# One shift per tile of patterns and Mish's first instruction on GpSimd, O in two buffers, and a newly planned order

## The chip, the cores and the metric

The kernel runs on one core of a Trainium2 chip. The metric is the device time of one execution in microseconds (us), the median of several runs. Five engines work in parallel, each in its own fixed order, held together by semaphores: TensorE (PE in the profile, PEld for its weight loads), VectorE (DVE), ScalarE (ACT), GpSimd (POOL) and SyncE (SP), which issues most DMAs.

## The reference

The input is a sequence of S = 2048 tokens of width D = 640. Two branches are computed from it and mixed by a gate for each token.

```python
def _A_ref(x, wqkv, wo):                      # attention, H = 32 heads of Dh = 20
    qkv = (x @ wqkv).reshape(B, S, 3, H, Dh)  # q, k, v: [B, H, S, Dh]
    scores = einsum("bhqd,bhkd->bhqk", q, k) * Dh ** -0.5
    p = softmax(scores, axis=-1)
    o = einsum("bhqk,bhkd->bhqd", p, v)
    return o.transpose(0, 2, 1, 3).reshape(B, S, D) @ wo

def _B_ref(x, w1, b1, w2):                    # dense layer with Mish, F = 1536
    h = einsum("bsd,df->bsf", x, w1) + b1
    act = h * tanh(softplus(h))
    return einsum("bsf,fd->bsd", act, w2)

g = sigmoid((x * gate_w).sum(-1, keepdims=True))
return g * a + (1 - g) * b
```

All inputs are bf16.

## The kernel before

**Blocks.** The attention weights are cut into blocks of 128 keys x 512 queries of one head. There are 32 heads x 16 key tiles x 4 query chunks = 2048 such blocks. PE computes a block of scores into PSUM (L1219); then the block has to go through an exponential, and PE multiplies it with V (L1456). Four heads of a group and a key tile make a *tile* of four blocks.

**Two ways to an exponential.** ACT takes two or three blocks in one instruction and writes bf16 (L1246: 128x1024 is a *pair*, 128x1536 a *triple*). DVE takes whole tiles. It turns each score into a 16-bit integer by one multiplication and addition (L1304, one instruction for each of four blocks), and those bits, read as a half-precision number, are a rough exponential. To make it a good one, three such *patterns* are summed with weights: two more copies of the tile are made by adding a constant to all its integers (L1334, one instruction of 128x2048 int16 for each copy; the text calls it a *shift*). PE multiplies the three patterns with V, with V x 161/128 and with V x 203/128. These two scaled sets of V are made by GpSimd (L1359, two instructions of 128x84 for each tile). So a tile of patterns costs DVE six instructions, and PE three passes over it in place of one.

**After a group.** When a group of four heads and a query chunk is done, DVE copies its output O with the sums of the softmax from PSUM into one buffer OUNG (L1551). The sums go by DMA to RR, are inverted there (L1558), and go by two more DMAs (L1559, L1561) to all partitions of BCT; then GpSimd multiplies O with them in four pieces of 128x128 (L1518). The next copy into OUNG waits for these.

**Mish.** The other branch runs in the background of the attention. For each of 24 pieces of 128x1024, ACT takes one tanh (L1013) and DVE does the rest in six instructions (L1033 to L1038): the *lift* (L1033, float32 to half precision), two cheap additions (L1034, L1036) and three products (L1035, L1037, L1038).

**What sets the order.** The Python code plans the whole program before it is built. A table of constants gives each kind of instruction a cost. The planner walks through steps (a step is one ACT exponential), and at each one decides from the planned clocks of the engines what every engine does next: whether a tile is taken for patterns (`start_tile`), which queue DVE serves (`work`: norm, soon, blend, bg), when PE does a background matmul. `STRETCHES` replaces some of the constants from given steps on. What comes out is one fixed list of instructions for each engine, with waits on semaphores; nothing is decided on the chip. At the start three of the four query chunks of x are loaded by transposing DMAs (L557), two ahead of the bulk of the weights (L582) and one behind them.

A second program, for inputs whose scores could leave the range of the patterns, is built too and not executed here.

Of the kernel before, what the change touches and what calls it, by code (L numbers as in the profile page):

```python
# [17 lines left out]
P = 128  # L18
# [41 lines left out]
HALVED = 0.41  # L60
# [7 lines left out]
Q_WAIT = 6  # L68
# [7 lines left out]
TIMES = 0.7  # L76
# [13 lines left out]
MISH = 1.7  # L90
# [4 lines left out]
FULL = 0.60  # L95
SCALED = 0.34
LIFT = 512.0
# [13 lines left out]
CALM = 6  # L111
PACKED = 17
# [18 lines left out]
SETS = 8  # L131
ULPS = 1024 / math.log(2)
BASE = 13680.1
SHADE = 0.61


STRETCHES = {
    13: {"EAGER": 144, "FMIN": 0.128, "FREE": 0.235, "SPUN": 0.495, "THIRD": 1.187, "VMIN": 1.48},
    33: {"EAGER": 144, "FMIN": 0.273, "FREE": 0.235, "SPUN": 0.495, "THIRD": 1.187, "VMIN": 1.48},
    53: {"CALLED": 7.573, "CALM": 3, "EAGER": 144, "FMIN": 0.332, "FREE": 0.235, "PATIENCE": 11.967, "ROOM": 2.116, "SPUN": 0.495, "THIRD": 1.187, "VMIN": 1.48, "XLATE": 10.107, "XSLACK": 0.076},  # L140
    74: {"AHEAD": 32, "CALLED": 7.573, "CALM": 8, "CROWD": 1.442, "EAGER": 144, "FMIN": 0.354, "FREE": 0.235, "NEED": 2, "OVER": 0.266, "PATIENCE": 3.941, "ROOM": 2.116, "SPUN": 0.467, "THIRD": 1.341, "VMIN": 1.48, "XLATE": 10.107, "XSLACK": 0.076},
    95: {"BUSY": 1.495, "CALLED": 2.701, "CROWD": 1.338, "FMIN": 0.33, "FREE": 0.173, "SPUN": 0.564, "STREAM": 0.496},
    116: {"CROWD": 1.454, "ROOM": 1.78, "STREAM": 0.464, "VMIN": 0.691, "XSLACK": 0.385},
    138: {"CROWD": 1.454, "EAGER": 159, "FREE": 0.15, "ROOM": 1.78, "STREAM": 0.464, "THIRD": 0.562, "VMIN": 0.691, "XSLACK": 0.385},
    159: {"XSLACK": 0.541},
    178: {"AHEAD": 13, "BEHIND": 21.412, "BUSY": 0.268, "CROWD": 1.246, "EAGER": 144, "FREE": 0.235, "MARGIN": 1.043, "OVER": 0.25, "PATIENCE": 12.851, "ROOM": 2.303, "XSLACK": 0.56},
    197: {"AHEAD": 17, "BEHIND": 13.21, "BUSY": 0.268, "CALLED": 2.332, "CALM": 9, "CROWD": 1.378, "EAGER": 144, "FMIN": 0.062, "FREE": 0.148, "LATER": 0.62, "MARGIN": 1.043, "OVER": 0.279, "PATIENCE": 8.968, "ROOM": 2.303, "XSLACK": 0.56},
    218: {"AHEAD": 17, "BEHIND": 13.21, "BUSY": 0.268, "CALLED": 2.332, "CALM": 9, "CROWD": 1.378, "EAGER": 156, "FMIN": 0.062, "FREE": 0.148, "KEPT": 14, "LATER": 0.62, "LOAD": 0.609, "MARGIN": 1.043, "OVER": 0.279, "PATIENCE": 13.444, "ROOM": 2.078, "STREAM": 0.365, "XLATE": 7.955, "XSLACK": 0.633},
    238: {"BUSY": 0.481, "EAGER": 131, "FMIN": 0.093, "LATER": 0.493, "LOAD": 0.49, "MARGIN": 0.871, "ROOM": 2.374, "XSLACK": 0.42},
    259: {"BUSY": 0.481, "CALLED": 1.571, "EAGER": 131, "FMIN": 0.065, "LATER": 0.493, "LOAD": 0.49, "MARGIN": 0.871, "NEED": 4, "OVER": 0.166, "ROOM": 2.345, "STREAM": 0.348, "VMIN": 2.036, "XSLACK": 0.42},  # L150
# [135 lines left out]
def bass_gated_mix__softmax_full_mha__dense_activation_mish__prompt_kernel(  # L286
# [39 lines left out]
    U2 = sb("U2", [P, 2 * CW], FP32)  # L326
    RR = sb("RR", [P, 16], FP32)
    BCT = sb("BCT", [P, CW], FP32)
    GATE = sb("GATE", [P, NTB], FP32)
    OMG = sb("OMG", [P, NTB], FP32)  # L330
    GT1 = sb("GT1", [P, NTB], FP32)
# [77 lines left out]
    def attention(pl, fast):  # L409
# [42 lines left out]
        def real(g):  # L452
            return min(g, NG - 1)
# [1553 lines left out]
```

## Time and profile before

| | |
|---|---|
| median of 3 runs | 752.26 us (752.16 to 753.0) |
| the profiled execution's own time | 752.22 us |
| its span | 750.3 us |
| mean granted clock of TensorE | 0.997 |
| DMA | 50.44 MB, mean 67 GB/s |
| work of the start (0 to 12 us) | ACT busy 6.47 us, DVE 5.02 us |
| the middle (32 to 700 us) | ACT busy 666.15 us, DVE 631.55, PE 653.19, POOL 187.32 |

A row of the groups reads: line, engine, operation, output <- inputs, (partitions x elements, type) and count | busy us, mean ns of one | idle time of the engine just before, and what ended it. Consecutive instructions of one engine overlap a little at their ends, so that a mean duration is somewhat longer than the distance from start to start. The busy time of PE is modelled, and 96% there does not mean that PE is at its peak.

### The profile page before, as it was taken

The page shows a single profiled execution, that of the slowest core. Times are in us where ns is not written, and L with a number is a line of the kernel's source. Part 1 is how long each engine was busy: PE and PEld are TensorE (multiplying, and loading weights), DVE is VectorE, ACT ScalarE, POOL GpSimd, SP SyncE. Part 2 cuts the span into 40 slices and gives each one's busy share as a digit, 9 for nine tenths or more (in the row PEclk, how much of TensorE's full clock was granted, in tenths as well). Part 3 has the DMA queues.
Part 4 walks back from the last instruction along what each step waited for, and adds up shares of the span by engine and source line. Part 5 has one row for each costly group of instructions (what it writes and reads, how often), then busy time and mean ns, then how long its engine had stood idle before and what let it go on. Part 6 is the DMA issues. An engine that isn't in the chain of part 4 may idle for free.

```text
span 750.3 us, 25694 instructions
## 1 busy us (share of the span) xinstructions
PE 721.5 (96%) x11307; PEld 274.8 (37%) x11307; DVE 689.9 (92%) x1203; ACT 732.8 (98%) x764; POOL 211.8 (28%) x399
## 2 busy tenths in 40 slices
PE   8899999999999999999989999999999999999996
PEld 3333334334423342233333433334444434333342
DVE  3698898999999999998999999999999999999986
ACT  6899999999999999999999999999999999999995
POOL 3203241312332213232213332212331243313142
PEclk9999999999999999999999999999999999999998
DMA  9402422132233313632132111111212212010001
GB/s 235 61 26 70 83 85 85 26 112 64 57 93 119 94 56 88 181 70 54 41 86 74 56 34 30 43 43 56 87 52 70 68 58 70 21 30 21 30 17 42
DMA packets 78015, 50.44 MB, mean 67 GB/s; under 512 B 21408, under 2 KB 73880, under 8 KB 77848
## 3 DMA queue, kind: packets, MB, share of 16 engines
q1 hardware_dynamic: 75528, 48.24, 23.3%
q8 instruction: 91, 1.49, 0.9%
q10 hardware_dynamic: 2256, 0.47, 0.3%
q14 instruction: 28, 0.23, 0.1%
q0 software_dynamic: 112, 0.01, 0.1%
HBM read 39.01 MB, written 8.90 MB: 64 GB/s over the span
## 4 chain that ended last, share of the span: by engine, by line
ACT 63%; PE 18%; DVE 11%; DMA 4%; SPq 1%; issue 1%; POOL 0%; DVEq 0%
ACT ETS L1246 62%; PE PS L508 6%; PE PS L1219 6%; PE PS L1456 5%; DVE LN L1304 3%; DVE LN L1334 2%; DMA XB<-in_A_x_dram 2%; SPq L557 1%; ACT REG L1013 1%; DMA W2R<-in_B_w_dram 1%; DMA BCT<-SUMS 1%; DVE REG L1304 1%; DVE HB L989 1%; DMA RR<-OUNG 1%; ACT W2R L1013 1%
## 5 line engine op out<-in xcount | busy, mean ns | idle before, releaser
L1246 ACT ACTIVATE ETS<-PS 128x1024 bf16<-128x1024 f32 (+1 forms) x733 | 711.2, 1158 | 3.8 <-PE PS L1219 3.1
L1219 PE MATMUL PS<-QT,KT 32*128 32x512 bf16 (+1 forms) x2128 | 287.6, 377 | 14.0 <-ACT ETS L1246 10.5
L1304 DVE TENSOR_SCALAR LN<-PS 128x512 int16<-128x512 f32 x396 | 266.1, 682 | 25.0 <-PE PS L1219 23.6
L1518 POOL TENSOR_TENSOR QT<-OUNG,BCT 128x128 bf16<-128x128 f32 x124 | 65.9, 562 | 481.6 <-DMA BCT<-SUMS 481.6
L1219 PEld LDWEIGHTS PS<-QT,KT 32*128 32x128 bf16 x2128 | 72.3, 91 | 238.9 <-ACT ETS L1246 211.5
L1359 POOL TENSOR_SCALAR VS<-V_all 128x84 bf16<-128x84 bf16 x262 | 138.9, 530 | 35.9 <-DVE V_all L836 8.0
L1456 PE MATMUL PS<-ETS,V_all 128*21 128x512 bf16 (+1 forms) x1596 | 148.0, 375 | 0.1
L1334 DVE TENSOR_SCALAR LN<-LN 128x2048 int16<-128x2048 int16 x182 | 126.1, 695 | 3.7 <-PE PS L1456 3.1
L508 PE MATMUL PS<-XB,REG 128*32 128x256 bf16 (+2 forms) x1800 | 87.2, 296 | 2.7 <-DVE LN L1304 1.8
L1456 PE MATMUL PS<-LN,VS 128*21 128x512 f16 (+1 forms) x832 | 78.7, 379 | 0.3
L508 PE MATMUL PS<-W2R,HB 128*32 128x320 bf16 x1536 | 74.4, 301 | 0.0
L1456 PEld LDWEIGHTS PS<-ETS,V_all 128*21 128x21 bf16 x1596 | 37.8, 90 | 50.4 <-issue 42.2
L508 PEld LDWEIGHTS PS<-XB,REG 128*32 128x32 bf16 (+1 forms) x1800 | 41.7, 96 | 29.9 <-issue 19.4
L508 PE MATMUL PS<-WOQ,QT 128*32 128x320 bf16 x1024 | 50.7, 301 | 0.6 <-DVE QT L1544 0.5
L508 PEld LDWEIGHTS PS<-W2R,HB 128*32 128x32 bf16 x1536 | 35.8, 96 | 24.2 <-issue 12.2
L1304 DVE TENSOR_SCALAR REG<-PS 128x512 int16<-128x512 f32 x60 | 40.1, 679 | 1.5 <-PE PS L1219 1.2
L1456 PE MATMUL PS<-LN,V_all 128*21 128x512 f16 (+1 forms) x408 | 38.7, 376 | 0.2 <-DVE OUNG L1551 0.2
L508 PE MATMUL PS<-XB,WOQ 128*32 128x512 bf16 (+2 forms) x440 | 35.5, 382 | 0.3 <-DVE LN L1304 0.3
L1456 PEld LDWEIGHTS PS<-LN,VS 128*21 128x21 bf16 x832 | 19.7, 89 | 39.9 <-issue 21.6
L989 DVE TENSOR_TENSOR HB<-PS,B1F 128x512 bf16<-128x512 f32 x48 | 32.6, 679 | 0.5 <-PE PS L508 0.4
L508 PEld LDWEIGHTS PS<-WOQ,QT 128*32 128x32 bf16 x1024 | 23.2, 96 | 17.3 <-issue 8.7
L1304 DVE TENSOR_SCALAR W2R<-PS 128x512 int16<-128x512 f32 x36 | 24.2, 682 | 0.6 <-PE PS L1219 0.6
(116 smaller groups left out, 496.8 us busy)
## 6 DMA issues: line engine op xcount, KB each, us to landing
REG<-in_B_w_dram SPq DMA_DIRECT2D x36, 320.0 KB, 3.3
BCT<-SUMS SPq DMA_DIRECT2D x31, 256.0 KB
W2R<-in_B_w_dram SPq DMA_DIRECT2D x12, 320.0 KB, 4.2
QT<-QS SPq DMA_DIRECT2D x28, 128.0 KB, 3.3
KT<-KS SPq DMA_DIRECT2D x28, 128.0 KB
KS<-LN SPq DMA_DIRECT2D x16, 128.0 KB, 3.4
QS<-WOQ SPq DMA_DIRECT2D x16, 120.0 KB
W2R<-in_B_w_dram SPq DMA_DIRECT2D x12, 160.0 KB, 3.8
```

Source lines behind the costliest of these rows:

```text
L508: last = e.matmul(to[at + j:at + j + n, :], w[:, j:j + n], x, start=start, stop=stop, tile_position=(0, at + j))
L557: "sp", lambda e: e.dma_start_transpose(xt(c), x_ap[c * CW:(c + 1) * CW, :]), (), f"xt{c}", cost=4.5, tail=3.6)]
L989: ev = dve(lambda e: e.tensor_tensor(hb, PS[:, bank, :].rearrange("p (i t) -> p i t", i=2), bias, ALU.add), [last, *b1f, *guarded, *b_read ...
L1013: ex = pl.add("act", lambda e: e.activation(U, h, AF.Tanh, bias=BEND, scale=0.5), [ev, u_free[0]], cost=0.94)
L1219: op = pl.add("pe", lambda e, to=to, g=real(g), tile=tile, j=j, cols=cols, c=c, of_q=of_q: e.matmul(to[:, cols], KT[32 * j:32 * j + 32, g, ...
L1246: e_op[s] = pl.add("act", lambda e: e.activation(RING[:, p:p + n, :], scores(s)[:, 0:n, :], AF.Exp, scale=SCALE), [s_op[s], *(pv_slot[b] f ...
L1304: bank_free[bank] = x_ops[bank] = tile["op"] = dve(lambda e: e.tensor_scalar(dst, PS[:, bank, :], SCALE * ULPS, BASE, ALU.mult, ALU.add), ...
L1334: op = pl.add("dve", lambda e: e.tensor_scalar(to, src, SHADES[n] - SHADES[held], None, ALU.add), [made, *deps], cost=SHADE)
L1359: weighted[(c, g, k)] = n, [pl.add("pool", lambda e, i=i, n=n, src=src: e.tensor_scalar(VS[:, n, i, :, :], src, WEIGHTS[i + 1], None, ALU. ...
L1456: lasts[n] = pl.add("pe", lambda e, v=v, j=j, src=src[:, cols], of_q=of_q, begin=begin, end=end: e.matmul(PS[32 * j:32 * j + EW, ACC, of_q ...
L1518: oung_free[0] = bc_read[0] = otn_done[(c, g)] = pl.add("pool", lambda e, some=some: e.tensor_tensor(otn(c, g)[:, some], src[:, some], BC[ ...
```

## The change

What it does:

- The second shift of each tile moves from DVE to GpSimd, as two instructions of 128x1024 (`GLOOM = 2`). The first stays on DVE. The patterns may now be made and used in either order.
- Mish's lift moves from DVE to GpSimd, in four pieces of 128x256 (`LIFTER = 1`). The other five instructions stay on DVE. GpSimd's work is put in order by a new function, `grind`.
- O is copied into two buffers of OUNG in turn.
- The sets of scaled V are 5 instead of 8. Some small tensors share memory.
- All three transposing loads of x go ahead of the bulk of the weights.
- The constants of the planner and all of `STRETCHES` are new, and with them the order of the program. It now takes 139 tiles for patterns (556 blocks) where it took 127 (508 blocks), and ACT's 733 exponentials are 707 pairs and 26 triples where they were 659 and 74.

```diff
-SETS = 8
+SETS = 5
+LIFTED = 0.43
+HOMES = {0: ('dve', 1024, FULL), 1: ('pool', 256, 0.4), 2: ('pool', 128, 0.27), 3: ('pool', 256, 0.69), 4: ('pool', 128, 0.42)}
+LIFTER, MILLER, ENDER = 1, 0, 0
+SPLIT = 1
+GLOOM = 2
+SHADOW = 2.25
...
-    OUNG = sb("OUNG", [P, CW], FP32)
+    OUNG = sb("OUNG", [P, 2, CW], FP32)
...
-            load_x(1)
-            load_x(2)
+            for c in range(1, NC):
+                load_x(c)
...
-            load_x(3)
...
+            def grind():
+
+                while gloom and pl.now["pool"] < pl.now["act"] + GRIST:
+                    if gloom[0][0]().t1 + HOP >= pl.now["act"] + AWAY:
+                        break
+                    gloom.popleft()[1]()
+                while mill and mill[0][0].t1 + HOP < pl.now["act"] + AWAY and pl.now["pool"] < pl.now["act"] + GRIST:
+                    mill.popleft()[1]()
...
+                    w = HG // count
+                    for i in range(count):
+                        some = slice(i * w, (i + 1) * w)
+                        op = pl.add(eng, lambda e, some=some: e.tensor_scalar(
+                            to[:, some, :], src[:, some, :], SHADES[n] - SHADES[held], None, ALU.add), [made, *deps], cost=cost)
...
-            for n in range(1, len(SHADES)):
-                piece(n)
+            if not GLOOM:
+                for n in range(1, len(SHADES)):
+                    soon.append((SHADE, piece(n, "dve", 1, SHADE), ready, due))
+            else:
+                soon.append((SHADE, piece(1, "dve", 1, SHADE), ready, due))
+                gloom.append((ready, piece(2, "pool", GLOOM, SHADOW / GLOOM + 0.1)))
...
-            while oung_free[0] == "busy":
+            m = oung_turn[0]
+            oung_turn[0] = 1 - m
+            while oung_free[m] == "busy":
                 (norm or lasting).popleft()[1]()
-            src = OUNG[:, :]
+            src = OUNG[:, m, :]
```

Of `STRETCHES` one line shows the kind of change:

```diff
-    546: {"OVER": 0.225, "ROOM": 1.348},
+    536: {"CROWD": 1.522, "FMIN": 0.103, "LATER": 0.57, "LOAD": 0.578, "XSLACK": 0.335},
```

In the changed kernel the lines are: exponential L1295, conversion to patterns L1353, shift L1388 (on both engines), scaled V L1420, copy of O L1621, scaling of O L1586, lift L1043, Mish's products L1044 and L1045, its additions L1048, its tanh L1029.

**On DVE, around the twelfth of the 24 pieces of Mish.** Before (U2 holds the half-precision numbers of Mish, LN and REG patterns):

```order
L1033 TENSOR_SCALAR U2<-REG 128x1024
L1304 TENSOR_SCALAR REG<-PS 128x512
L1034 TENSOR_SCALAR U2<-U2 128x1024
L1075 SCALAR_TENSOR_TENSOR REG<-PS,GATE,XS 128x320
L1035 TENSOR_TENSOR U2<-U2 128x1024
L1334 TENSOR_SCALAR LN<-LN 128x2048
L1036 TENSOR_SCALAR U2<-U2 128x1024
L1304 TENSOR_SCALAR LN<-PS 128x512
L1037 TENSOR_TENSOR U2<-U2 128x1024
L1075 SCALAR_TENSOR_TENSOR REG<-PS,GATE,XS 128x320
L1038 TENSOR_TENSOR HB<-U2,HB 128x1024
```

And now:

```order
L1048 TENSOR_SCALAR U2<-U2 128x1024
L1353 TENSOR_SCALAR LN<-PS 128x512
L1044 TENSOR_TENSOR U2<-U2 128x1024
L1048 TENSOR_SCALAR U2<-U2 128x1024
L1353 TENSOR_SCALAR LN<-PS 128x512
L1124 SCALAR_TENSOR_TENSOR REG<-PS,GATE,XB 128x320
L1005 TENSOR_TENSOR HB<-PS,B1F 128x512
L1353 TENSOR_SCALAR LN<-PS 128x512
L1044 TENSOR_TENSOR U2<-U2 128x1024
L1353 TENSOR_SCALAR LN<-PS 128x512
L1621 COPY OUNG<-PS 128x512
```

The lift at the head is gone from DVE, and conversions from PSUM (L1353) stand where shifts and the lift stood.

**On GpSimd, between two scalings of O in the middle of the program.** Before:

```order
L1518 TENSOR_TENSOR QT<-OUNG,BCT 128x128 x4
L1359 TENSOR_SCALAR VS<-V_all 128x84 x8
L1518 TENSOR_TENSOR QT<-OUNG,BCT 128x128 x4
L1359 TENSOR_SCALAR VS<-V_all 128x84 x10
L1518 TENSOR_TENSOR QT<-OUNG,BCT 128x128 x4
```

And now:

```order
L1586 TENSOR_TENSOR QT<-OUNG,BCT 128x128 x4
L1388 TENSOR_SCALAR REG<-LN 128x1024 x2
L1420 TENSOR_SCALAR VS<-V_all 128x84 x2
L1388 TENSOR_SCALAR LN<-LN 128x1024 x2
L1420 TENSOR_SCALAR VS<-V_all 128x84 x2
L1388 TENSOR_SCALAR REG<-LN 128x1024 x2
L1420 TENSOR_SCALAR VS<-V_all 128x84 x2
L1388 TENSOR_SCALAR LN<-LN 128x1024 x2
L1420 TENSOR_SCALAR VS<-V_all 128x84 x2
L1043 TENSOR_SCALAR U<-REG 128x256 x4
L1388 TENSOR_SCALAR LN<-LN 128x1024 x2
L1420 TENSOR_SCALAR VS<-V_all 128x84 x2
```

Where GpSimd had eight or ten small instructions in one piece and then waited for the next scaling of O, it now has two large shifts between each two small ones, and the scaling of O stands in line behind them.

**On ACT, from the fourteenth tanh of Mish on** (all rows but L1013 and L1029 are exponentials). Before:

```order
L1013 ACTIVATE REG<-HB 128x1024
L1246 ACTIVATE ETS<-PS 128x1024 x3
L1246 ACTIVATE ETS<-PS 128x1536
L1246 ACTIVATE ETS<-PS 128x1024
L1246 ACTIVATE ETS<-PS 128x1536
L1246 ACTIVATE ETS<-PS 128x1024 x3
L1246 ACTIVATE ETS<-PS 128x1536
L1246 ACTIVATE ETS<-PS 128x1024 x10
L1013 ACTIVATE REG<-HB 128x1024
```

And now:

```order
L1029 ACTIVATE REG<-HB 128x1024
L1295 ACTIVATE ETS<-PS 128x1024 x47
L1029 ACTIVATE REG<-HB 128x1024
L1295 ACTIVATE ETS<-PS 128x1024 x15
L1029 ACTIVATE REG<-HB 128x1024
```

The triples are gone from this part; only pairs are left.

More of the change, by code (lines that the diff above doesn't have):

```diff
@@ L111 @@
 CALM = 6
+HANG = 2.0
 PACKED = 17
@@ new lines, in plus @@
+                def plus(s):
+                    return lambda e, at: e.tensor_scalar(B[:, at], A[:, at], 1 / LIFT, s, ALU.mult, ALU.add)
+                chains.append((ex, due, [
+                    (*HOMES[LIFTER], lift, taken), ("dve", 2 * CW, SCALED, plus(a - 2), None), (*HOMES[MILLER], times, None),
+                    ("dve", 2 * CW, SCALED, plus(b - c), None), (*HOMES[MILLER], times, None), (*HOMES[ENDER], last, done)]))
+                if len(chains) == 1:
+                    onward(ex, 0)
@@ L1470, in sets @@
             for tile in off_tiles.get(queue[0][2][:2], ()):
[L1471 removed]
+                n += sum(op.t1 + HOP <= pl.now["pe"] for op, *_ in tile["items"][tile["given"]:])
             return n
```

243 lines of the change are left out of this document (138 added, 105 removed).

## The prediction

> **What bounds the kernel now.** First the page's busy times, then its chain of work that ended last.
>
> ```profile
> span 750.3 us, 25694 instructions
> PE 721.5 (96%) x11307; PEld 274.8 (37%) x11307; DVE 689.9 (92%) x1203; ACT 732.8 (98%) x764; POOL 211.8 (28%) x399
> ...
> ACT 63%; PE 18%; DVE 11%; DMA 4%; SPq 1%; issue 1%; POOL 0%; DVEq 0%
> ```
>
> ACT is busy for all but 17.5 us of the span, and most of the chain runs on it. So the time is the sum of ACT's instructions plus a start and an end. DVE has some 60 us free, GpSimd more than 500. The groups of instructions with their shapes kept apart say what ACT's time is made of:
>
> ```profile
> L1246 ACT ACTIVATE ETS<-PS 128x1024 bf16<-128x1024 f32 x659 | 624.8, 1115 | 3.0 <-PE PS L1219 2.2 <-PE PS L1456 0.2
> L1246 ACT ACTIVATE ETS<-PS 128x1536 bf16<-128x1536 f32 x74 | 113.1, 1540 | 0.9 <-PE PS L1219 0.9
> ```
>
> A triple takes 1.540 us, a pair 1.115, and ACT waited less than 4 us for work. What ACT does not take, DVE must take as patterns, so the change buys ACT time with DVE time, and DVE time with GpSimd time. The waits of the engines show how much lateness lies between DVE and ACT:
>
> ```profile
> PEld PS L1219 <- ACT ETS L1246: 211.5, 583, 1.3
> ...
> DVE LN L1304 <- PE PS L1219: 23.6, 54, 2.7
> ...
> ACT ETS L1246 <- PE PS L1219: 3.1, 6, 1.0
> ```
>
> PE, which stands between them, waited 583 times for ACT to free a PSUM bank, 0.36 us on average. A delay of PE by DVE that is shorter than this does not reach ACT.
>
> **The change, part by part.** The working is against the profiled execution: 752.22 us, of which 750.3 are its span and 1.9 lie around it. That is the median of the runs (752.26).
>
> *ACT.* There are 733 exponentials as before, but 48 triples have become pairs. Each saves 1.540 - 1.115 = 0.425 us, so 48 x 0.425 = **20.4 us**, all on the path. With nothing else changed this gives 752.2 - 20.4 = 731.8 us.
>
> *DVE.* It gets 48 more conversions and loses 115 shifts (254 to 139) and the 24 lifts:
>
> ```profile
> L1304 DVE TENSOR_SCALAR LN<-PS 128x512 int16<-128x512 f32 x396 | 266.1, 682 | 25.0 <-PE PS L1219 23.6
> L1334 DVE TENSOR_SCALAR LN<-LN 128x2048 int16<-128x2048 int16 x182 | 126.1, 695 | 3.7 <-PE PS L1456 3.1
> L1033 DVE TENSOR_SCALAR U<-REG 128x1024 f16<-128x1024 f32 x18 | 12.3, 682 | 0.0
> L1033 DVE TENSOR_SCALAR U<-W2R 128x1024 f16<-128x1024 f32 x6 | 4.6, 760 | 0.0
> ```
>
> That is 48 x 0.682 = 32.7 more, 115 x 0.695 = 79.9 and 12.3 + 4.6 = 16.9 less: 689.9 - 64.1 = 625.8 us of work.
>
> *PE.* Twelve more tiles of three passes instead of one are 24 passes of four matmuls. A row of the timeline (start, duration) gives what one costs:
>
> ```profile
> 300.70 0.40 PE L1456 MATMUL PS<-LN,VS 128*21 128x512 f16 x4
> ...
> 300.93 0.39 PE L1456 MATMUL PS<-LN,V_all 128*21 128x512 f16 x4
> ```
>
> They start 0.23 us apart, so this is 5.5 us, hidden by the 211.5 us in which PE waits for ACT. Without that cover it would be 5.5 us.
>
> *GpSimd.* The trace has no shift there. These rows have the nearest things:
>
> ```profile
> L1359 POOL TENSOR_SCALAR VS<-V_all 128x84 bf16<-128x84 bf16 x262 | 138.9, 530 | 35.9 <-DVE V_all L836 8.0
> ...
> L591 POOL COPY WOQ<-WOQ 128x400 bf16<-128x400 bf16 x1 | 0.5, 517 | 3.5 <-DMA WOQ<-in_A_wqkv_dram 3.5
> ...
> L607 POOL COPY REG<-GW 128x5 bf16<-128x5 bf16 x1 | 0.2, 207 | 4.0 <-DMA GW<-in_gate_w_dram 4.0
> ...
> L1874 POOL TENSOR_TENSOR HB<-LN,W2R 128x320 bf16<-128x320 f32 x1 | 0.9, 857 | 7.8 <-ACT LN L1872 7.8
> ```
>
> ```profile
> L1359 POOL TENSOR_SCALAR VS<-V_all x262: 417/418/1441, 17.3 to 735.7; 128x84 bf16<-128x84 bf16 x131
> ...
> L1518 POOL TENSOR_TENSOR QT<-OUNG,BCT x124: 447/457/1178, 57.0 to 733.6; 128x128 bf16<-128x128 f32 x124
> ```
>
> ```profile
> 145.87 1.70 POOL L1518 TENSOR_TENSOR QT<-OUNG,BCT 128x128 bf16<-128x128 f32 x4 [10.75 <-DMA BCT<-SUMS]
> 147.66 0.92 POOL L1359 TENSOR_SCALAR VS<-V_all 128x84 bf16<-128x84 bf16 x2
> ```
>
> The two copies differ by 395 elements and 310 ns: 0.785 ns for an element of one input. The 128x84 instruction takes 418 ns at its median, so 418 - 84 x 0.785 = 352 ns of it are fixed. A half shift is then 0.352 + 1024 x 0.785 ns = 1.16 us, and 1.24 from start to start (a pair of the small ones in the third fence: 0.92 - 0.42 = 0.50, which is 0.08 more than one takes). The other end is the slope of the two-input instruction, (857 - 457) / 192 = 2.1 ns, which gives 2.58 us. The shift has one input, so I take 1.24. A lift of 128x256 by the same rule is 0.63. GpSimd's sum: 278 x 1.24 = 345, 282 small ones x 0.50 = 141, 124 scalings x 0.42 = 52, 96 lifts x 0.63 = 61, some 10 at the start: **609 us**, 83% of the new span. It fits, with 120 us to spare.
>
> *DVE against GpSimd.* The two engines get in each other's way. The groups of line 1334 and two pairs of rows of the timeline:
>
> ```profile
> L1334 DVE TENSOR_SCALAR W2R<-W2R x12: 676/684/990, 48.3 to 272.3; 128x2048 int16<-128x2048 int16 x12
> ```
>
> ```profile
> 673.85 0.97 DVE L1334 TENSOR_SCALAR REG<-REG 128x2048 int16<-128x2048 int16 x1
> ```
>
> ```profile
> 673.81 0.46 POOL L1518 TENSOR_TENSOR QT<-OUNG,BCT 128x128 bf16<-128x128 f32 x1 [15.69 <-DMA BCT<-SUMS]
> ```
>
> ```profile
> 606.22 0.68 DVE L1334 TENSOR_SCALAR LN<-LN 128x2048 int16<-128x2048 int16 x1
> ```
>
> ```profile
> 606.05 0.95 POOL L1359 TENSOR_SCALAR VS<-V_all 128x84 bf16<-128x84 bf16 x1
> ```
>
> At 673.8 a shift that begins just behind a scaling of O takes 0.97 instead of 0.68: it waits 0.29 us, about 128 elements at 2.1 ns. At 606 the small instruction had begun 0.17 us ahead of the shift; the shift is not delayed, but GpSimd takes 0.95 instead of 0.42. So one waits for the other only while elements move, not in GpSimd's fixed part, and a half shift holds DVE back for up to 1024 x 0.785 ns = 0.80 us.
>
> The Trainium skill ("SBUF — State Buffer", § SBUF: two separate sides) says that these engines share a port pair as an exclusive lock, and that whoever starts first holds it for the whole instruction. The rows agree with the exclusion; the pair at 606 disagrees with "starts first" and with "whole". By that rule GpSimd would hold the ports for 278 x 1.16 + 282 x 0.42 + 124 x 0.46 + 96 x 0.55 = 550 us, DVE would lose 84 us instead of the 34 worked out next, and the sum would be some 744 us; the sum goes by the rows.
>
> GpSimd moves elements for 278 x 0.80 + 124 x 0.29 + 96 x 0.20 + 282 x 0.07 = 297 us, 41% of 730. A DVE instruction that comes at a random moment waits with that chance, on average for 0.32 us (half of what it hits, most of it 0.80). DVE has 139 shifts, 48 additions and 72 products of Mish that can be held up: 259 x 0.41 x 0.32 = **34 us**. So DVE works 625.8 + 34 = 660 of 730 us, and has 70 us free where it had 60: it is no tighter than before. What reaches ACT is the part of a wait that exceeds PE's 0.36 us. Of 259 x 0.41 = 106 waits spread over 0 to 0.80 us this is 0.12 us each, 13 us if PE needs every delayed result at once, and nothing if the planner left slack everywhere. I take **5 us**, since a shift is mostly followed by conversions into banks that PE needs later.
>
> *New waits.* Mish's first addition on DVE now waits for GpSimd's lift, whose four pieces take 4 x 0.63 = 2.5 us instead of 0.68; 24 times 1.8 us of lateness in background work, with nothing behind it that is due at once. A shift on DVE that writes over the tile it came from waits until GpSimd has read that tile; conversions stand behind it, and PE waits for those: this is what the upper end of 13 us is for. The scalings of O wait for a DMA at the head of GpSimd's queue, and now shifts stand behind them:
>
> ```profile
> POOL QT L1518 <- DMA BCT<-SUMS: 481.6, 31, 28.0
> ```
>
> Before, nothing stood behind those 31 waits that was due. If each still costs 1 us, 31 us of the 120 spare ones are gone, and nothing of ACT's time.
>
> *Small parts.* The second buffer of O saves one wait, and covers the scalings that now stand behind shifts; 0 to -0.8 us, taken as 0:
>
> ```profile
> DVE OUNG L1551 <- POOL QT L1518: 0.8, 1, 0.8
> ```
>
> The third load of x goes ahead of three issues of weights on SP (first fence, SP's timeline). The chain at the start waits for its arrival (second fence):
>
> ```profile
> 10.04 0.58 SPq L582 DMA_DIRECT2D REG<-in_A_wqkv_dram  x1
> 10.66 0.53 SPq L582 DMA_DIRECT2D WOQ<-in_A_wqkv_dram  x1
> 11.23 0.75 SPq L582 DMA_DIRECT2D REG<-in_A_wqkv_dram  x1
> ```
>
> ```profile
> 12.03 12.70 DMA XB<-in_A_x_dram
> ```
>
> 0.58 + 0.53 + 0.75 = 1.9: it can gain up to 1.9 us, and lose as much if the weights come late; taken as 0. Fewer sets of V only mean that they are made just before they are used; GpSimd's spare time covers this.
>
> **Sum:** 752.2 - 20.4 + 5 = 736.8 us. With the bounds (-1.9 - 0.8 at the start and the buffer, 0 to 13 for the waits): 729 to 745.
>
> **Rivals.**
>
> 1. *DVE becomes the bound, and the kernel is slower.* Both shifts of a tile wait for the same fourth conversion, so DVE's and GpSimd's start together, and each of the 139 would meet a half shift in full: 139 x 0.80 = 111 us, and 120 x 0.41 x 0.32 = 16 for Mish. DVE would need 626 + 127 = 753 us beside the 15 us of the first 32 in which it has no work yet:
>
> ```profile
> 0.00:12.00 12.00, 8.75 (x128) 4.14 (x132) 5.02 (x12) 6.47 (x9) 5.85 (x11) 1.00 1.01 190
> 12.00:32.00 20.00, 18.02 (x268) 7.57 (x264) 11.57 (x20) 18.38 (x20) 6.16 (x13) 1.00 0.72 163
> ```
>
> (The third pair of numbers is DVE: 5.02 of 12 us and 11.57 of 20.) It decides at a mean wait of 0.43 us: 626 + 259 x 0.43 + 15 = 752 us. For it speaks that rows such as the one at 673.8 exist; against it that in the new order of DVE a shift stands between conversions, so that its turn is rarely the very moment at which its tile is ready. At 0.46 us, with the 1.9 us around the span: 626 + 119 + 15 + 2 = about **762 us**. The Trainium skill ("Perfetto Trace Analysis", § Optimizing Scalar/DVE Operations) warns in the same sense that moving work between these two engines might not help because of the shared port.
>
> 2. *GpSimd becomes the bound.* With c for a half shift its sum is 264 + 278 c. At c = 1.6 this is 709 us, beside its own waits for DVE (those of the 0.95 us kind, some 30 us) more than the span. The third pattern then comes late for PE, and PE's fixed order stops ACT. At c = 1.8: 264 + 500 + 30 = 794 us. For it: the slope of 2.1 ns in the row of L1874. Against it: that row has two inputs.
>
> 3. *Most of the gain is eaten.* The waits come as single delays up to 0.8 us, and PE's fixed order passes them on more often than I take: the 13 us, and 3 more where GpSimd's third pattern comes late. 731.8 + 16 = **748 us**, still faster.
>
> 4. *Nothing comes of it:* the 20.4 us come back as waits of ACT for PE, 752 us.
>
> **How the numbers follow.** My forecast (729 to 745) gets 0.60, rival 3 0.14, rival 4 0.05, rival 1 0.13, rival 2 0.08. About 0.2%, 1.5 us, is what a measurement of this kernel can tell from no change. Faster by more: 0.60 + 0.14 = 0.74; the same: 0.05; slower: 0.21. The range that holds 8 in 10 takes the forecast, rival 3 and rival 4: 729 to 753.
>
> **What would show it.** Right: about 707 pairs at 1.115 us and ACT busy for some 712 us; half shifts on POOL at 1.1 to 1.3 us and POOL at 80 to 90%; L1388 on DVE with a median near 0.69 and a maximum near 1.5; DVE's busy time, waits included, 645 to 675. Wrong by rival 1: a mean of L1388 on DVE above 1.1 us and PE waiting for DVE. Wrong by rival 2: POOL above 95% and PE waiting for POOL at L1524. Wrong altogether: ACT waiting for PE for more than 20 us.

## The result and the profile after

| | before | after |
|---|---|---|
| median | 752.21 us (752.16 to 753.0) | 1147.64 us (1145.2 to 1150.45) |
| ratio | | 1.5254, 95% interval 1.5217 to 1.5291 |
| profiled execution: span | 750.3 us | 1143.2 us |
| mean granted clock of TensorE | 0.997 | 0.824 |

The prediction, 736.8 us in a range of 729 to 753, was wrong, in sign as well as in size. The page of the changed kernel begins with the busy times:

```profile
span 1143.2 us, 26026 instructions
PE 883.3 (77%) x11376; PEld 297.3 (26%) x11377; DVE 705.8 (62%) x1112; ACT 749.2 (66%) x764; POOL 1028.7 (90%) x795
```

ACT has gone from 98% of the span to 66%, GpSimd (POOL) from 28% to 90%. The groups say with what, and the durations of one group (minimum/median/maximum in ns, first and last start) how long one is:

```profile
L1388 POOL TENSOR_SCALAR LN<-LN 128x1024 int16<-128x1024 int16 x170 | 480.0, 2841 | 25.6 <-DVE LN L1353 25.4 <-PE PS L1524 0.2
L1420 POOL TENSOR_SCALAR VS<-V_all 128x84 bf16<-128x84 bf16 x282 | 145.6, 516 | 23.9 <-DVE V_all L851 1.6
L1586 POOL TENSOR_TENSOR QT<-OUNG,BCT 128x128 bf16<-128x128 f32 x124 | 57.8, 495 | 0.1
```

```profile
L1388 POOL TENSOR_SCALAR LN<-LN x170: 2760/2772/3286, 30.4 to 1095.1; 128x1024 int16<-128x1024 int16 x170
```

A half shift takes **2.77 us**, not 1.24. The 170 of this group are most of the 278; all of them need 278 x 2.77 = 770 us. The waits show how that reaches ACT:

```profile
ACT ETS L1295 <- PE PS L1268: 365.2, 279, 6.6
PEld PS L1524 <- POOL LN L1388: 216.7, 94, 6.0
DVE LN L1353 <- PE PS L1268: 203.1, 210, 6.3
PE PS L1524 <- POOL LN L1388: 187.6, 88, 5.7
```

Read from below: PE comes to the third pattern of a tile, finds it unfinished and waits, up to 6 us at a time. Its order is fixed, so the next scores come late, and ACT waits 365 us for them where it waited 3. (The two rows of PE overlap: the weight load and the multiplication wait for the same pattern.) A stretch in the middle has GpSimd full and every other engine with holes; the columns are window, then PE, PEld, DVE, ACT and POOL busy, the granted clock, the share of DMA and GB/s:

```profile
500.00:600.00 100.00, 74.56 (x980) 23.30 (x975) 57.84 (x93) 64.12 (x67) 97.78 (x72) 0.85 0.14 36
```

This is rival 2. Three things stay open behind it: why a half shift costs so much, whether anything else in the change is at fault (the new order, contention, the clock of 0.82), and whether the forecast would have held at the price it assumed.

### The profile page after: what moved, and what is told of

Read it like the earlier page. It is cut to its first block, busy times and chain, and to the rows that moved or that the text cites. A ratio compares the mean times of both kernels' runs of the same rounds, so it can differ in the third digit from the quotient of the medians.

```text
span 1143.2 us, 26026 instructions
## 1 busy us (share of the span) xinstructions
PE 883.3 (77%) x11376; PEld 297.3 (26%) x11377; DVE 705.8 (62%) x1112; ACT 749.2 (66%) x764; POOL 1028.7 (90%) x795
## 3 DMA queue, kind: packets, MB, share of 16 engines
q8 instruction: 91, 1.49, 0.6%
## 5 line engine op out<-in xcount | busy, mean ns | idle before, releaser
L1295 ACT ACTIVATE ETS<-PS 128x1024 bf16<-128x1024 f32 (+1 forms) x733 | 725.4, 1042 | 369.3 <-PE PS L1268 365.2
L1388 POOL TENSOR_SCALAR LN<-LN 128x1024 int16<-128x1024 int16 x170 | 480.0, 2841 | 25.6 <-DVE LN L1353 25.4
L1353 DVE TENSOR_SCALAR LN<-PS 128x512 int16<-128x512 f32 x436 | 296.8, 685 | 206.2 <-PE PS L1268 203.1
L1268 PE MATMUL PS<-QT,KT 32*128 32x512 bf16 (+1 forms) x2122 | 332.4, 437 | 4.3 <-ACT ETS L1295 1.7
L1524 PE MATMUL PS<-LN,VS 128*21 128x512 f16 (+1 forms) x888 | 94.9, 452 | 188.2 <-POOL LN L1388 187.6
L1524 PE MATMUL PS<-ETS,V_all 128*21 128x512 bf16 (+1 forms) x1556 | 169.6, 443 | 0.0
L1420 POOL TENSOR_SCALAR VS<-V_all 128x84 bf16<-128x84 bf16 x282 | 145.6, 516 | 23.9 <-DVE V_all L851 1.6
L1388 DVE TENSOR_SCALAR LN<-LN 128x2048 int16<-128x2048 int16 x91 | 82.8, 913 | 45.9 <-POOL LN L1388 25.7
L522 PE MATMUL PS<-XB,REG 128*32 128x256 bf16 (+1 forms) x1800 | 107.5, 345 | 0.8 <-DVE LN L1353 0.6
L1524 PEld LDWEIGHTS PS<-LN,VS 128*21 128x21 bf16 x888 | 18.9, 91 | 237.0 <-POOL LN L1388 216.7
L1388 POOL TENSOR_SCALAR REG<-LN 128x1024 int16<-128x1024 int16 x28 | 79.5, 2856 | 1.0 <-DVE LN L1353 1.0
L1388 POOL TENSOR_SCALAR LN<-REG 128x1024 int16<-128x1024 int16 x24 | 66.9, 2802 | 0.2 <-DVE REG L1353 0.2
L1388 POOL TENSOR_SCALAR LN<-W2R 128x1024 int16<-128x1024 int16 x20 | 56.5, 2842 | 4.0 <-DVE W2R L1353 4.0
L1586 POOL TENSOR_TENSOR QT<-OUNG,BCT 128x128 bf16<-128x128 f32 x124 | 57.8, 495 | 0.1
L522 PEld LDWEIGHTS PS<-XB,REG 128*32 128x32 bf16 x1800 | 46.7, 107 | 41.1 <-issue 30.2
L1524 PEld LDWEIGHTS PS<-ETS,V_all 128*21 128x21 bf16 x1556 | 39.0, 95 | 61.2 <-issue 55.4
L1353 DVE TENSOR_SCALAR W2R<-PS 128x512 int16<-128x512 f32 x52 | 35.2, 684 | 31.8 <-PE PS L1268 31.6
L1524 PE MATMUL PS<-LN,V_all 128*21 128x512 f16 (+1 forms) x444 | 48.8, 434 | 0.0
```

Source lines behind the costliest of these rows:

```text
L522: last = e.matmul(to[at + j:at + j + n, :], w[:, j:j + n], x, start=start, stop=stop, tile_position=(0, at + j))
L1268: op = pl.add("pe", lambda e, to=to, g=real(g), tile=tile, j=j, cols=cols, c=c, of_q=of_q: e.matmul(to[:, cols], KT[32 * j:32 * j + 32, g, ...
L1295: e_op[s] = pl.add("act", lambda e: e.activation(RING[:, p:p + n, :], scores(s)[:, 0:n, :], AF.Exp, scale=SCALE), [s_op[s], *(pv_slot[b] f ...
L1353: bank_free[bank] = x_ops[bank] = tile["op"] = dve(lambda e: e.tensor_scalar(dst, PS[:, bank, :], SCALE * ULPS, BASE, ALU.mult, ALU.add), ...
L1388: op = pl.add(eng, lambda e, some=some: e.tensor_scalar(to[:, some, :], src[:, some, :], SHADES[n] - SHADES[held], None, ALU.add), [made, ...
L1420: ops = [pl.add("pool", lambda e, i=i, n=n, src=src: e.tensor_scalar(VS[:, n, i, :, :], src, WEIGHTS[i + 1], None, ALU.mult), [v_done[(rea ...
```

## The experiments

Three theories for the 395 us. T1: the price of the half shift is all. T2: DVE and GpSimd get in each other's way. T3: the rest of the change (order, buffers, lift) or the clock. Medians of kernels in experiments are of four runs each, beside seven of the kernel before.

### What an instruction of GpSimd costs by itself

A kernel of single instructions, each form three times alone, then beside a DVE that never stops.

> The computation of the reference is left out; single GpSimd instructions of chosen forms are timed, first alone, then beside a busy DVE. T1 (the form is dear: a 16-bit integer TENSOR_SCALAR takes 2.5 ns for each element, whatever else runs): the shift of 128x1024 int16 takes 2.7 to 2.8 us alone, 128x512 1.49, 128x2048 5.3, and at most 0.2 us more beside DVE; the same shift done as an int32 addition of pairs (512 elements) 1.2 to 1.3 us; a bf16 TENSOR_SCALAR of 1024 elements 2.7 us like the int16 one, the float32 to float16 one about 1.0 us. T2 (the two engines get in each other's way): the shift of 128x1024 takes 1.2 us alone, by the copies' slope, and 2.5 us or more beside DVE. T3 (something else in the changed kernel): 1.2 us in both.

The groups of the part without DVE:

```profile
L25 POOL TENSOR_SCALAR T<-A 128x2048 int16<-128x2048 int16 x3 | 16.0, 5371 | 0.0
L32 POOL TENSOR_SCALAR T<-AF 128x1024 f16<-128x1024 f32 x3 | 8.3, 2797 | 0.0
L32 POOL TENSOR_SCALAR T<-ABF 128x1024 bf16<-128x1024 bf16 x3 | 8.3, 2793 | 0.0
L25 POOL TENSOR_SCALAR T<-A 128x1024 int16<-128x1024 int16 x3 | 8.2, 2772 | 0.0
...
L25 POOL TENSOR_SCALAR T<-A 128x512 int16<-128x512 int16 x3 | 4.4, 1491 | 0.0
L28 POOL TENSOR_TENSOR T<-A,CP 128x512 int32<-128x512 int32 x3 | 3.0, 1053 | 0.0
L35 POOL COPY T<-ABF 128x1024 bf16<-128x1024 bf16 x3 | 3.0, 1073 | 0.0
```

The shift takes 2.77 us with nothing beside it: (5371 - 1491) / 1536 = 2.53 ns an element. T1 has its price, and a copy of the same size takes 1.07. Three parts were missed. Pairs took 1.05 us, not 1.2 to 1.3. Beside DVE a half shift takes 3.29 us on average, half a microsecond more and not at most 0.2. And float32 to half precision also takes 2.80, where 1.0 was expected from the kernel's lift (0.40 us for 256 elements). The lift differs in having two operations. So the number of operations was varied:

```diff
-e.tensor_scalar(to, src, -342, None, ALU.add)              # one
+e.tensor_scalar(to, src, -342, 0, ALU.add, ALU.add)        # two additions
+e.tensor_scalar(to, src, 1.0, -342, ALU.mult, ALU.add)     # times, plus
```

> The computation of the reference is left out; single GpSimd instructions are timed, alone and then beside a busy DVE. The lift of the changed kernel is a TENSOR_SCALAR with two operations (times, plus) and took 0.40 us for 256 elements, 0.77 ns each; the one-operation TENSOR_SCALARs of the first run of single instructions took 2.5 ns an element in int16, bf16 and float32. If the number of operations sets the price (T1a): the int16 shift written with a second operation that adds 0 takes 1.0 us for 128x1024 and 0.3 for 128x128, bf16 and float32 alike, and with one operation 2.77 again. If something else in the lift does (T1b, its scalars or its place): 2.5 ns an element in all of them.

> The computation of the reference is left out; single GpSimd instructions are timed, alone and then beside a busy DVE. So far one operation (times or plus) took 2.5 ns an element in every type, two additions 3.4, times and plus 0.75 in bf16 and float32. If the pair of operations sets the price (T1a): the int16 shift written as times 1.0, plus -342 takes 0.28 to 0.32 us for 128 elements, 1.0 to 1.1 for 1024, 1.9 for 2048. If int16 is dear in any form (T1c): 2.77 us or more for 1024.

The second kernel (two additions on int16; times and plus on bf16 and float32), then the third (times and plus on int16):

```profile
L25 POOL TENSOR_SCALAR T<-A 128x2048 int16<-128x2048 int16 x3 | 21.2, 7086 | 0.0
...
L25 POOL TENSOR_SCALAR T<-A 128x512 int16<-128x512 int16 x3 | 5.7, 1922 | 0.0
L35 POOL TENSOR_SCALAR T<-ABF 128x1024 bf16<-128x1024 bf16 x3 | 3.1, 1047 | 0.2
```

```profile
L25 POOL TENSOR_SCALAR T<-A 128x2048 int16<-128x2048 int16 x3 | 5.7, 1901 | 0.2
...
L25 POOL TENSOR_SCALAR T<-A 128x512 int16<-128x512 int16 x3 | 1.9, 620 | 0.2
```

Two additions cost (7086 - 1922) / 1536 = 3.36 ns an element, times and plus (1901 - 620) / 1536 = **0.83**. The first expectation (two operations, hence cheap) failed; it is the pair "times, plus" that is cheap, in each of the three types tried.

### The changed kernel with a cheaper half shift

First as an int32 addition of two 16-bit numbers at a time, then with two additions, then as times 1.0, plus the difference. The order of every engine is that of the changed kernel.

```diff
+a, b = (x[:, some, :].bitcast(I32)... for x in (to, src))
+op = pl.add(eng, lambda e: e.tensor_tensor(a, b, both.to_broadcast([P, pairs]), ALU.add), ...)
```

> The changed kernel with the same order on every engine; only the 278 half shifts on GpSimd become int32 additions of two 16-bit numbers at a time (512 elements for 1024). T1 (the price of the form is all): 1.26 us for a half shift (the lift's fixed 0.2 us and 2.1 ns for each of 512 elements of two inputs), GpSimd's sum 278 x 1.26 + 141 + 56 + 38 + 10 = 595 us, and the time is ACT's again: 730 to 748 us. T2 (contention on the port sets the time): GpSimd is busy longer than 900 us and the time stays above 950. T3 (the new order, the second buffer of O, the lift or the clock): the time stays above 1000, since all of these are left as they are.

> The changed kernel with the same order on every engine; the half shifts on GpSimd have a second operation that adds 0. T1a: 1.0 us for a half shift, GpSimd's sum 278 x 1.0 + 245 = 523 us, and the time falls from 1148 to 769 us or less (the run with pairs, where a half shift took 1.18 us); if the length of the half shifts holds the 33 us between that run and the forecast of 737, nearer to 750; if not, 765 to 770. T1b: 2.77 us and 1148 us again.

> The changed kernel with the same order on every engine; the half shifts on GpSimd are written as times 1.0, plus the difference. T1a: 1.05 us for a half shift (my price was 1.16 for its length), GpSimd's sum some 278 x 1.1 + 245 = 550 us, and the time is 755 to 769 us: below the run with pairs (769.3; 1.18 us and two inputs to read) by what the shorter shifts free, above the forecast of 737 by what the order costs. If the price alone was wrong in the prediction: 730 to 745. T1c: 1148 or more.

| half shift on GpSimd | one, alone | median | against before |
|---|---|---|---|
| plus (the change) | 2.77 us | 1147.64 us | 1.5254 (1.5217 to 1.5291) |
| two additions | 3.63 | 1381.14 | 1.8365 (1.8302 to 1.8427) |
| int32 pairs | 1.05 | 769.3 | 1.0233 (1.0216 to 1.0251) |
| times, plus | 1.05 | 769.93 | 1.0234 (1.0217 to 1.0251) |

One form of one instruction takes the time from 1148 to 770 us, or up to 1381. (The 3.63 and the last 1.05 are the means of three instructions of 1024 elements alone, in the second and the third kernel of single instructions.) The order, the buffers and the lift are the same in all four, so they account for none of these 378 us. T2 makes a small part of them at most: with times and plus DVE's shifts are still held up, as is shown below, and the time is 770. The granted clock goes with PE's busy share, 0.756 at 69%, 0.824 at 77% and 0.997 at 96% in the last two rows, so its fall comes with the dear half shift; how much of the 378 us goes through the slower clock was not separated. The run with two additions came out as neither of its expectations had it (769 or less, or 1148), the pairs missed their 730 to 748, and times and plus just missed its 755 to 769. So 770 is neither the forecast of 737 nor faster than before.

### Without the half shifts on GpSimd

```diff
-GLOOM = 2
+GLOOM = 0        # both shifts on DVE
-LIFTER, MILLER, ENDER = 1, 0, 0
+LIFTER, MILLER, ENDER = 0, 0, 0        # second kernel: the lift too
```

> The changed kernel with both shifts of a tile on DVE as before, Mish's lift still on GpSimd; the order is planned anew and has 614 pairs, 116 triples and 118 tiles of patterns (before: 659, 74, 127). T1: no half shift is left on GpSimd, so ACT bounds it: 752 - 45 x 0.904 + 42 x 1.33 = 767 us (start to start of a pair and a triple in the trace of before), 760 to 775. T2: 760 to 775 too, since little is left on GpSimd to contend. T3 (the lift, the buffer or the constants are to blame): above 850.

> As the run with both shifts on DVE, and the lift back on DVE too: of the change there are left the second buffer of O, five sets of V instead of eight, the third load of x moved ahead and the constants of the planner; 619 pairs, 110 triples, 120 tiles. T1 and T2: ACT bounds it, 752 - 40 x 0.904 + 36 x 1.33 = 764 us, 757 to 772. T3 (buffer, sets, constants): above 850; with the lift alone to blame, far below the run with both shifts on DVE.

Measured were 768.43 us (1.0214, 1.0197 to 1.0231) and 773.5 (1.028, 1.0263 to 1.0297). The first is ACT's bound for its plan (767). The second is 9.5 us above its own (764) and outside its range; there is no shift on GpSimd in it, its trace has ACT waiting 8.1 us for PE at L1524, and why was not followed up. Neither is near 850, so the buffers, the sets, the lift and the constants do not make the bulk. The order of both is planned anew, so they say nothing of the changed kernel's order; the four kernels above do.

### What makes the other 33 us: 770 against 737

T4: the half shifts still do harm, by holding DVE up or by coming late. T5: the new order cannot reach ACT's bound. To tell them apart, the half shifts got almost no elements to move, in the form with two additions first:

```diff
+width = slice(0, 32 if eng == "pool" and at in written else CW)
-to[:, some, :], src[:, some, :],
+to[:, some, width], src[:, some, width],
```

> The run with two operations, and each half shift on GpSimd does 64 elements instead of 1024 (except where it writes a buffer for the first time), so that most of the third pattern is left out of the computation; the order on every engine is the same, all waits stay, the price of a shift on GpSimd is about 0.26 us. T4 (what is left over 737 us comes from the half shifts: DVE kept waiting while they move elements, and PE waiting for them): 730 to 745 us, DVE's own shifts at 0.70 on average, DVE busy for some 630 us. T5 (it comes from the new order on PE, ACT and DVE, which does not reach ACT's bound even with shifts that cost nothing): 755 to 770.

The median was 763.52 us (1.0136, 1.0099 to 1.0174), as T5 has it. But the run misleads: a buffer's first pattern was still made whole, at 3.6 us for each half, and the first 100 us show what that did there:

```profile
0.00:100.00 100.00, 85.31 (x1090) 32.13 (x1090) 60.96 (x104) 78.33 (x83) 53.92 (x72) 0.95 0.36 81
...
300.00:400.00 100.00, 96.20 (x1294) 31.20 (x1286) 84.33 (x146) 93.16 (x102) 55.18 (x101) 0.95 0.28 78
```

ACT is busy for 78 of the first 100 us, and for 93 from 300 to 400, where one more buffer is written for the first time; in the run that follows it is 93 and 100. So it was repeated with times and plus:

> As the run with times and plus, and each half shift on GpSimd does 64 elements instead of 1024 except where it writes a buffer for the first time, so that most of the third pattern is left out of the computation (the run with short shifts again, without the dear form in its first 80 us, which cost ACT some 13 us there). T4 (the half shifts cause what is left over 737): 730 to 742 us. T5 (the new order causes it): 747 to 760, that is 763 less what the first 80 us lost.

741.08 us (0.9859, 0.9842 to 0.9875): T4. T5 and the reading of the run before it fall. The pages of the whole half shifts (times, plus) and of the short ones:

```profile
span 769.2 us, 26026 instructions
PE 738.6 (96%) x11376; PEld 281.9 (37%) x11377; DVE 682.5 (89%) x1112; ACT 722.8 (94%) x764; POOL 576.0 (75%) x795
```

```profile
span 738.8 us, 26026 instructions
PE 721.8 (98%) x11376; PEld 276.9 (37%) x11377; DVE 646.4 (87%) x1112; ACT 713.7 (97%) x764; POOL 341.4 (46%) x795
```

DVE works 36.1 us longer beside whole half shifts, and the span is 30.4 us longer. DVE's groups have the place, whole first, then short:

```profile
L1388 DVE TENSOR_SCALAR LN<-LN 128x2048 int16<-128x2048 int16 x91 | 76.9, 848 | 2.3 <-PE PS L1525 1.3 <-PE PS L1268 0.6
L1044 DVE TENSOR_TENSOR U<-U 128x1024 f16<-128x1024 f16 x48 | 40.2, 838 | 0.2
```

```profile
L1390 DVE TENSOR_SCALAR LN<-LN 128x2048 int16<-128x2048 int16 x91 | 64.3, 711 | 2.2 <-PE PS L1528 1.8
L1044 DVE TENSOR_TENSOR U<-U 128x1024 f16<-128x1024 f16 x48 | 33.4, 696 | 0.2
```

With whole half shifts, DVE's shifts and Mish's products take 0.14 us longer on average, and Mish's additions 0.18 (0.620 against 0.443), while its conversions from PSUM stay at 0.68 in both. That could still go with late patterns. The next kernel keeps the length of a half shift, but moves a third of the elements:

```diff
+width = slice(0, 168 if part else CW)        # part: one operation, 2 x 168 elements
```

> The run with times and plus, the same order on every engine, but each half shift on GpSimd is a one-operation instruction over 336 elements instead of 1024 (207 + 336 x 2.5 ns = 1.05 us, the same length), except where it writes a buffer for the first time, so that two thirds of the third pattern are left out of the computation. T4a (DVE is held up while elements move: the one-operation form held it 0.83 us for 1024 elements): a third of the elements, so a third of the 29 us: 748 to 754 us, DVE's shifts at 0.74 on average. T4b (the length of the half shifts, by a late third pattern and GpSimd's queue, makes the 29 us): 766 to 772.

744.66 us (0.9896, 0.988 to 0.9913), even below T4a's 748 to 754. A half shift takes 1.19 us on average in this kernel and in the one with whole half shifts. So at this length GpSimd's time and the lateness of its patterns cost next to nothing (3.6 us, the hold of the remaining third included), and some 25 of the 29 us come from elements that move while DVE wants to.

### Attempts to shorten the hold

With the small instructions for V cheaper (times, plus 0.0), with four pieces of 512 for two of 1024, with both, and with one-operation int32 additions of pairs:

```diff
-VS[:, n, i, :, :], src, WEIGHTS[i + 1], None, ALU.mult)
+VS[:, n, i, :, :], src, WEIGHTS[i + 1], 0.0, ALU.mult, ALU.add)
...
-GLOOM = 2
+GLOOM = 4
...
+a, b, by = a.bitcast(I32), b.bitcast(I32), by * 65536 + by
```

> As the run with times and plus, and the 282 small instructions that weight V are written as times, plus 0.0 too: 0.28 us instead of 0.42 each, 40 us less on GpSimd, V's sets ready earlier. If PE's waits for V's sets (6 us in the run with pairs) reach ACT: 3 to 6 us less than the run with times and plus; if not: within 2 us of it.

> The run with times and plus, the whole computation; the third pattern is made on GpSimd in four pieces of 512 elements instead of two of 1024, in the same place in its order; nothing else moves. A piece takes 0.62 us, a tile 2.5 instead of 2.1, so GpSimd's sum grows by 139 x 0.4 = 53 us to some 630. T4a: DVE is held up for 0.42 us at most instead of 0.83, its 36 us of waits become 18 to 25, and the time falls to 755 to 764. T4b: the third pattern comes 0.4 us later and GpSimd has more to do, 770 to 785.

> As the run with four pieces, with the weights of V as times, plus 0.0 (0.30 us instead of 0.42), which gives GpSimd 40 us back. T4a: GpSimd is ready sooner and meets DVE's shifts more often, which cost 4 us with two pieces (774.4 against 769.9): with four pieces half of that, 757 to 766, not below the run with four pieces. T4b: less queue, 3 to 10 us below the run with four pieces.

> The changed kernel with the same order on every engine; a half shift on GpSimd is one-operation int32 addition over 512 elements, two 16-bit numbers in each, with one input (the run with pairs had two), and V's weights are times, plus 0.0. At 2.5 ns an element a half shift takes 0.207 + 512 x 2.5 ns = 1.49 us, GpSimd's sum is some 278 x 1.6 + 190 = 630 us. If the hold is counted by elements of one input (0.83 us for 1024): at most 0.41 us for DVE, its shifts at 0.76 to 0.80 on average (0.86 in the run with times and plus, 0.88 with the weights changed too), and the time is 750 to 763: what DVE gains the later third pattern partly takes back (PE waiting for GpSimd 15 to 25 us). If the hold goes by the length of the instruction: DVE's shifts at 0.95 or more, 775 to 790.

| half shifts (GpSimd's weights of V) | median | against before | L1388/L1391 on DVE, mean of LN<-LN |
|---|---|---|---|
| two of 1024 | 769.93 us | 1.0234 (1.0217 to 1.0251) | 0.848 us |
| two of 1024 (cheap weights) | 774.37 | 1.0296 (1.0279 to 1.0313) | 0.914 |
| four of 512 | 767.82 | 1.0208 (1.0191 to 1.0225) | 0.812 |
| four of 512 (cheap weights) | 762.73 | 1.0143 (1.0125 to 1.0161) | 0.819 |
| two of 512 wide (cheap weights) | 783.08 | 1.0413 (1.0393 to 1.0433) | 0.795 |

All four expectations missed in part. Cheaper weights with two pieces make the kernel *slower*: DVE's shifts are held longer (0.914 us), probably because GpSimd is ready earlier (its waits for DVE's patterns at LN rose from 64 to 96 us) and meets them more squarely. Four pieces hold DVE up less, as T4a says, but gained 2 us and not 6 to 15, and with cheap weights they came out 5 us below, which T4b has and T4a does not. The wide elements hold DVE's shifts as little as expected (0.795 us, against 0.914 with the same weights), but the time rose by 9 us instead of falling. What takes the gain back is read from the waits, not tested by itself: those of the run with four pieces, where GpSimd is busy for 82%,

```profile
PEld PS L1525 <- POOL LN L1388: 19.9, 41, 1.6
...
PE PS L1525 <- POOL LN L1388: 7.5, 16, 1.3
```

and those of the run with wide elements, whose half shifts take 1.49 us at their median:

```profile
PEld PS L1527 <- POOL LN L1391: 41.7, 63, 2.7
ACT ETS L1295 <- PE PS L1268: 30.2, 60, 2.6
PE PS L1527 <- POOL LN L1391: 23.1, 39, 2.4
```

In all, weight loads and multiplications of PE wait for GpSimd for 46 and 84 us there; with times and plus it was 10, with a third of the elements 11, and with four pieces and cheap weights, the best of these, 20. Lateness, which cost next to nothing at 1.05 us a half and 77%, is back in both, at 82%. What shortens the hold lengthens the work. No version that computes everything came below the kernel before; the best, 762.73 us, is 1.4% above it.

## Why the prediction was wrong

**The step that failed** is the price of the half shift: "418 - 84 x 0.785 = 352 ns of it are fixed", and from it 1.16 us, 1.24 from start to start. The slope of two copies was put upon a TENSOR_SCALAR, and what it left over was called fixed. The rows quoted there had the answer the other way round. With the 5-element copy's 207 ns as the fixed part, 418 - 207 = 211 ns for 84 elements are 2.51 ns each, and 0.207 + 1024 x 2.51 ns = 2.78 us; measured 2.77. The row of the same operation was given the slope of another one.

**The range was too narrow for the same reason.** The upper end of 2.58 us stood in the text and was not carried into the range ("the shift has one input, so I take 1.24"). Rival 2's own formula, 264 + 278c, gives 264 + 278 x 2.77 = 1034 us of GpSimd's work; its busy time is 1028.7, and with 114 us of waits that is the span. The mechanism, its place (PE waiting for POOL at L1524) and its sum were right. Its chance of 0.08 was too small, and "POOL above 95%" was too strict a sign: it was 98% in the middle, 90% over the span.

**ACT's term held.** Predicted were 707 pairs and 20.4 us less. The first and last start of an exponential before, and with short half shifts, where its exponentials wait for scores for only 1.6 us:

```profile
L1246 ACT ACTIVATE ETS<-PS x733: 1016/1125/1676, 8.2 to 740.0; 128x1024 bf16<-128x1024 f32 x165, 128x1536 bf16<-128x1536 f32 x19
```

```profile
L1296 ACT ACTIVATE ETS<-PS x733: 1015/1086/1591, 8.3 to 720.0; 128x1024 bf16<-128x1024 f32 x179, 128x1536 bf16<-128x1536 f32 x5
```

The last one starts 20.0 us earlier. In the same run the whole kernel is only 11 us shorter than before, because of **a term that was missing**: the end. ACT's last instruction waits for PE, 2.5 us before, and now

```profile
ACT LN L1948 <- PE PS L522: 11.7, 1, 11.7
```

From the last start to the end of the span it was 750.3 - 740.0 = 10.3 us, and is 738.8 - 720.0 = 18.8. The changed kernel has it too (18.7), the two kernels that were planned anew do not (9.8). PE has background products left when the exponentials are done: in the last 18 us of this run are 256 passes of the output projection, 9.5 us; in the last 10 of the kernel before there were 36. Why the new order leaves them to the end was not tested.

```profile
L522 PE MATMUL PS<-WOQ,QT 128*32 128x320 bf16 x256 | 9.5, 300 | 0.4 <-issue 0.3
```

**DVE against GpSimd: the waits were larger than priced, and most of them reached the end.** 34 us were predicted for DVE from all that GpSimd moves, some 25 of them from the half shifts (222 of the 297 us), and the two runs, which differ in the half shifts alone, are 36.1 apart. DVE's own work was put too low as well: 625.8 us were predicted, and 646.4 are left with short half shifts; the cause of these 20 us was not followed up. Together DVE works 682.5 us and not 660.

What turned the sign at the assumed price is "5 us reach ACT": 769.93 - 741.08 = 28.8 do. It was argued that a delay under PE's 0.36 us of waiting for ACT is absorbed, one by one. The chains of work that ended last show that it is not (whole, then short half shifts):

```profile
PE 53%; DVE 32%; ACT 11%; issue 2%; DMA 0%
```

```profile
PE 57%; ACT 36%; DVE 5%; issue 1%; DMA 0%
```

With whole half shifts a third of the chain runs on DVE, with short ones a twentieth. PE still waits 165 us for ACT with whole half shifts, so that cover is not used up; that it does not lie where the delays are is argued. DVE's idle time is no room for them either: of its 769.2 - 682.5 = 86.7 us, some 73 are waits for PE. In the middle DVE is nearly full, so one delay is passed on to the next instruction; this last step is argued from the windows (whole, then short half shifts), not tested by itself:

```profile
600.00:700.00 100.00, 96.55 (x1618) 37.52 (x1614) 97.27 (x153) 94.80 (x101) 81.81 (x116) 1.00 0.19 56
```

```profile
600.00:700.00 100.00, 99.88 (x1753) 38.68 (x1745) 94.74 (x164) 99.99 (x110) 52.86 (x126) 1.00 0.18 50
```

**The sum as it should have been:** 752.2 - 20.4 (ACT) + 8.5 (the end) = 740.3, measured 741.1 with short half shifts; from there + 28.8 (whole half shifts, some 25 of it by elements moved) = 769.9 at the price assumed; + 377.7 (the price) = 1147.6. The last two terms are differences of measured medians. At the assumed price, then, the sign would have been wrong too. Rival 1 had 762 us for that case, but with 119 us of holds that bring DVE to its limit; they are 36, and DVE is busy for 89%. Its time was near by luck.

**Smaller points.** The lift on GpSimd was priced at 0.63 us and takes 0.404 at its median, for it is a "times, plus". DVE's shifts were held up by 0.88 us at most (maximum 1.56), as predicted, though the half shift beside them lasts more than twice as long as thought (2.77 us, not 1.16):

```profile
L1388 DVE TENSOR_SCALAR LN<-LN x91: 677/773/1562, 35.9 to 1118.4; 128x2048 int16<-128x2048 int16 x91
```

The Trainium skill ("SBUF — State Buffer", § SBUF: two separate sides) has the shared port locked for the whole instruction; with 2.77 us beside a maximum of 1.56 the trace disagrees on "whole". It also says that an instruction of DVE with two inputs from SBUF contends with GpSimd's reads, and there the trace agrees: Mish's products, 0.838 against 0.696 us.

## What to carry to other kernels

Price a moved instruction from a row of the same operation *and the same number of operations*, and take the fixed part from the smallest instruction on that engine; if two ends of a price lie on both sides of the point at which the engine becomes the bound, measure it or carry both into the range. Idle time of an engine is not room for delays when it lies at the start, at the end and where the engine waits for others. When ACT's work shrinks, look at what is left for PE after the last exponential.

## What was not expected of the hardware

- GpSimd's TENSOR_SCALAR costs 2.5 ns an element with one operation (int16, bf16 and float32 alike), 3.4 with two additions (int16), and 0.83 with "times, plus": doing more takes a third of the time. The Trainium skill ("GPSIMD Engine Reference", § 3.1 Elementwise — side-by-side cycle accounting) gives 1.03 cycles an element for bodies of k up to 2, which I read as the number of operations, and 1.2 GHz with it, an estimate of 0.86 ns. "Times, plus" agrees; one operation and two additions do not.
- A one-operation half shift of 2.77 us holds DVE for 0.83 us only, about what the elements would take at 0.83 ns each. In the first kernel of single instructions a DVE shift of 0.69 us takes 1.51 beside it:

```profile
82.65 1.51 DVE L74 TENSOR_SCALAR U<-D 128x2048 int16<-128x2048 int16 x1
```

"Times, plus", 1.05 us alone, holds DVE for as long. In the third kernel three of DVE's shifts take 4.41 us beside it and 1.88 when nothing holds them, 0.84 less for each:

```profile
58.79 4.41 DVE L77 TENSOR_SCALAR U<-D 128x2048 int16<-128x2048 int16 x3
...
68.11 1.88 DVE L77 TENSOR_SCALAR U<-D 128x2048 int16<-128x2048 int16 x3
```

- The exclusion can also fall on GpSimd alone. A little later in the third kernel GpSimd begins a one-operation half shift beside a DVE that is already busy without a gap. DVE is not held at all (three shifts in 1.88 us); GpSimd's instruction takes 14.80 us instead of 2.77, and ends 2.6 us after DVE's last one. Why it went this way here, and the other way in the first kernel, is not known; it was seen once:

```profile
72.40 1.88 DVE L77 TENSOR_SCALAR U<-D 128x2048 int16<-128x2048 int16 x3
```

```profile
71.02 14.80 POOL L28 TENSOR_SCALAR T<-A 128x1024 int16<-128x1024 int16 x1 [4.30 <-DVE U L77]
```

- The hold goes by elements moved: with a third of them at the same length DVE's shifts fell from 0.848 to 0.757 us on average, with half of them (wide, cheap weights) in 1.49 us instead of 1.05 from 0.914 to 0.795.
